# First stage of a SiLU MLP forward and backward: how the first 512 rows of x reach their transposed tile, and which queue loads the first slices of w1

## The chip, the cores and the metric

One NeuronCore of a Trainium2 chip runs the kernel. TensorE (PE) multiplies 128x128 weight tiles with up to 512 moving columns into PSUM; VectorE (DVE), ScalarE (ACT) and GpSimd (POOL) work beside it; SyncE (SP) does no arithmetic here and issues DMAs. A DMA can be issued from SP's queue or from ScalarE's. The metric is the device time of one execution in microseconds (us), the median of several runs, lower being better. Times inside the kernel are counted from the start of the profiled span.

## What is computed

x is 2048 x 640 (S x D), w1 is 640 x 1536 (D x F), w2 is 1536 x 640, all bf16. The reference is the forward pass and its gradients by x, w1 and w2 for a given grad_out:

```python
h = x @ w1
a = silu(h)
out = a @ w2
# and, from grad_out:
ga  = grad_out @ w2.T
gh  = ga * silu'(h)
gx  = gh @ w1.T
gw1 = x.T @ gh
gw2 = a.T @ grad_out
```

## The kernel before, in words

The rows are worked in NCH = 4 chunks of SC = 512. For a chunk the kernel needs x transposed (`xT`, 128 partitions x 5 blocks of D x 512 rows) and grad_out transposed (`goT`). With 128 of the 1536 columns of F as one group, `h_group` (L226) forms h with five matmuls (one for each block `dt_` of D, L206), takes silu (`silu_a`, L215, ScalarE), and prepares the derivative (`silu_grad`: tanh on ScalarE, L219, then two VectorE instructions, L221 and L222). `g_group` (L250) does the same for grad_out with w2 transposed. `sd_phase` (L264) multiplies back to D: w2 with a for `out`, w1 transposed with gh for `gx`. Intermediate results go to DRAM and come back transposed by DMA (`store_rows`, `load_a_blk`), and after the chunks the weight gradients gw2 (L357) and gw1 (L406) are accumulated over all rows. All of that is as it was.

What matters here is the first stage, chunk 0. Its order is this:

- **Warm-up.** `warm` is filled by VectorE (L141) and NWARM = 22 matmuls of 128 columns run on it (L145), before any data has come.
- **Loads on SP's queue, in this order.** Two loads of 256 rows of x each, whole rows, into `x_two` (`load_x_half`, L173, 320 KB each); w1's first 512 columns (the first of three slices of F) in three pieces, rows 0 to 127, rows 128 to 255 and the other three blocks (`load_w1_rows`, L178: 128, 128 and 384 KB); the second and third slice of w1 (`load_w1`, L169, 640 KB each); all of w2 (L186, 1920 KB); then DMA transposes of grad_out (L162), w2 (L189) and w1 (L190).
- **`start_before_entry_wait` (L16).** The instructions named in `early` (the warm-up, the two loads of x and the first two of w1), with all that stands ahead of them on their engine, are moved in front of the wait with which each engine enters the program proper. Each engine signals its arrival before them, so another engine does not wait for them.
- **ScalarE's table load.** A first activation of one column (L185) makes ScalarE load its function table.
- **Transposes on TensorE.** `pe_x_half` (L192) turns each half of the 512 rows: for each of the five blocks of D two transposes (L197) into one PSUM tile, then one copy to `xT` (L199), on VectorE for even `dt_` and on ScalarE for odd ones. Rows were loaded two to a partition, so the copy spreads them with a stride. In all 20 transposes and 10 copies.
- **`h_first` (L232).** For the first four groups (FB = 4, the first slice of w1) the first KM = 2 blocks of D are multiplied ahead, block by block over the four groups; then each of these groups is completed with the remaining blocks, and the other eight groups follow, five matmuls each. The fifth group is the first to need the second slice of w1. Each group's silu follows it, its tanh LAG_G = 4 groups later in the text.
- **Then** `sd_phase` with w2 and `aT`, the twelve `g_group`s of chunk 0 and `sd_phase` with w1T.

PSUM has eight buffers under one tag (`hp`), taken in turn by the warm-up tile, the transposed pieces and the groups. [...] The tanh result has three buffers (`tpool`), each freed by the VectorE instruction that reads it (L221).

The program's order on an engine can differ from the text, since a scheduler places instructions.

Of the kernel before, what the change touches and what calls it, by code (L numbers as in the profile page):

```python
# [9 lines left out]
ACT = mybir.ActivationFunctionType  # L10
# [5 lines left out]
def start_before_entry_wait(nc, names):  # L16

    def move(nc):
        blocks = nc.m.functions[0].blocks
        entry, home = blocks[0].instructions, blocks[1].instructions
        for engine in {i.engine for i in home if i.name in names}:
            mine = [i for i in home if i.engine == engine]
            last = max(k for k, i in enumerate(mine) if i.name in names)
            moved = mine[: last + 1]
            gate = next(
                k
                for k, i in enumerate(entry)  # L30
                if i.engine == engine and isinstance(i, mybir.InstEventSemaphore)
            )
            taken = {i.name for i in moved}
            for k in reversed(range(len(home))):
                if home[k].name in taken:
                    del home[k]
            for i in reversed(moved):
                entry.insert(gate, i)

    nc.at_finalize(move)  # L40
# [22 lines left out]
def kernel(  # L63
# [11 lines left out]
    nc = tc.nc  # L75
    P = 128
    x2 = x.flatten_outer_dims()
# [5 lines left out]
    S, D = x2.shape  # L83
    F = w1.shape[1]
    ST, DT, FT = S // P, D // P, F // P
    SC = 512
    NCH = S // SC
    STC = SC // P
    FC = 512
# [1 line left out]
    FB = FC // P  # L91
    LAG = 2
    LAG_G = 4
    KM = 2
    NWARM = 22
    dt_in = x.dtype

    dram = ctx.enter_context(tc.tile_pool(name="dram", bufs=1, space=bass.MemoryType.DRAM))
# [13 lines left out]
    w1_v = w1.rearrange("(dt p) f -> p dt f", p=P)  # L112
    w2_v = w2.rearrange("(ft p) d -> p ft d", p=P)
    x_v = x2.rearrange("(st p) d -> p st d", p=P)
# [17 lines left out]
    with ExitStack() as mctx:  # L132
        cpool = mctx.enter_context(tc.tile_pool(name="cpool", bufs=1))
# [6 lines left out]
        warm = cpool.tile([P, P], dt_in, name="warm")  # L140
        early = [nc.vector.memset(warm[:], 1.0)]  # L141
        warm_a = cpool.tile([P, 1], FP32, name="warm_a")
        wp = ps_h.tile([P, SC], FP32, name="wp", tag="hp")
        for i in range(NWARM):
            early.append(nc.tensor.matmul(wp[:, 0:P], lhsT=warm[:], rhs=warm[:], start=True, stop=True))  # L145

        ident = cpool.tile([P, P], dt_in, name="ident")
        make_identity(nc, ident[:])

        w1_nat = w1pool.tile([P, DT, F], dt_in, name="w1_nat", tag="w1a")  # L150
# [4 lines left out]
        def load_xT(c):  # L155
            xT = xpool.tile([P, DT, SC], dt_in, name="xT")
            nc.sync.dma_start_transpose(out=xT[:], in_=x2[c * SC:(c + 1) * SC, :])
            return xT
# [4 lines left out]
            return goT  # L163

        xT_next = xpool.tile([P, DT, SC], dt_in, name="xT")
        x_two = cpool.tile([P, 2, 2, D], dt_in, name="x_two")

        def load_w1(lo, hi):
            nc.sync.dma_start(out=w1_nat[:, :, lo:hi], in_=w1_v[:, :, lo:hi])  # L169

        def load_x_half(half):
            lo = half * 2 * P
            return nc.sync.dma_start(  # L173
                out=x_two[:, half, :, :], in_=x2[lo:lo + 2 * P, :].rearrange("(p q) d -> p q d", q=2)
            )

        def load_w1_rows(lo, hi):
            return nc.sync.dma_start(out=w1_nat[:, lo:hi, 0:FC], in_=w1_v[:, lo:hi, 0:FC])  # L178

        early += [load_x_half(0), load_x_half(1), load_w1_rows(0, 1), load_w1_rows(1, KM)]  # L180
        load_w1_rows(KM, DT)
        start_before_entry_wait(nc, {i.ins.name for i in early})
        for fc in range(1, NFC):
            load_w1(fc * FC, (fc + 1) * FC)
        nc.scalar.activation(warm_a[:], warm[:, 0:1], ACT.Silu)  # L185
        nc.sync.dma_start(out=w2_nat[:], in_=w2_v[:])  # L186
        goT_next = load_goT(0)
        for fc in range(NFC):
# [1 line left out]
        nc.sync.dma_start_transpose(out=w1T[:], in_=w1[:, :])  # L190

        def pe_x_half(xT, half):  # L192
            lo = half * 2 * P
            for dt_ in range(DT):
                tp = ps_h.tile([P, 2, P], dt_in, name="tp", tag="hp")
                for q in range(2):
                    nc.tensor.transpose(tp[:, q, :], x_two[:, half, q, dt_ * P:(dt_ + 1) * P], ident[:])  # L197
                copy = nc.scalar.copy if dt_ % 2 else nc.vector.tensor_copy
                copy(out=xT[:, dt_, lo:lo + 2 * P].rearrange("p (s q) -> p q s", q=2), in_=tp[:])  # L199

        pe_x_half(xT_next, 0)
        pe_x_half(xT_next, 1)

        def h_mm(hp, ft, xT, lo, hi):
            for dt_ in range(lo, hi):
                nc.tensor.matmul(  # L206
                    hp[:],
                    lhsT=w1_nat[:, dt_, ft * P:(ft + 1) * P],
                    rhs=xT[:, dt_, :],
                    start=(dt_ == 0),  # L210
                    stop=(dt_ == DT - 1),
                )
# [19 lines left out]
        def h_first(xT, aT, ghT):  # L232
            hps = []
            for ft in range(FB):
                hps.append(ps_h.tile([P, SC], FP32, name="hp"))
            for dt_ in range(KM):
                for ft in range(FB):
                    h_mm(hps[ft], ft, xT, dt_, dt_ + 1)
            for i in range(FT + LAG_G):
                if i < FT:  # L240
                    if i < FB:
                        h_mm(hps[i], i, xT, KM, DT)
                    else:
# [40 lines left out]
        for c in range(NCH):  # L284
            xT, goT = xT_next, goT_next
# [3 lines left out]
            if c + 1 < NCH:  # L289
                xT_next = load_xT(c + 1)  # L290
# [8 lines left out]
            if c == 0:  # L299
                h_first(xT, aT, ghT)  # L300
                nc.sync.dma_start(
                    out=aT_scr[:, c * SC:(c + 1) * SC].rearrange("(ft p) s -> p ft s", p=P), in_=aT[:]
                )
                sd_phase(c, w2_nat, aT, oT_scr)
                for ft in range(FT):
                    g_group(ft, goT, ghT)
                nc.sync.dma_start(
                    out=ghT_scr[:, c * SC:(c + 1) * SC].rearrange("(ft p) s -> p ft s", p=P), in_=ghT[:]
# [4 lines left out]
            for i in range(FT + LAG):  # L313
# [7 lines left out]
                out=aT_scr[:, c * SC:(c + 1) * SC].rearrange("(ft p) s -> p ft s", p=P), in_=aT[:]  # L321
            )
            nc.sync.dma_start(
                out=ghT_scr[:, c * SC:(c + 1) * SC].rearrange("(ft p) s -> p ft s", p=P), in_=ghT[:]
# [7 lines left out]
    with ExitStack() as fctx:  # L332
# [45 lines left out]
        for fc in range(NFC):  # L378
            gh_blk = gh_blks[fc]
            for dt_ in range(DT):  # L380
                if dt_ == DT // 2:
                    store_gw2(fc)
                if fc == NFC - 1 and dt_ == DT - 1:
                    for k, (lo, hi) in enumerate(((0, FC - P), (FC - P, FC))):
# [12 lines left out]
                        else:  # L397
                            nc.vector.tensor_copy(out=g1[:, lo:hi], in_=gp[:, lo:hi])  # L398
                        last_store = nc.sync.dma_start(
                            out=gw1_v[:, dt_, fc * FC + lo:fc * FC + hi], in_=g1[:, lo:hi]  # L400
# [49 lines left out]
```

## Time and profile before

| what | value |
|---|---|
| median of 5 runs | 320.91 us (320.52 to 321.57) |
| the profiled execution, its own time | 320.68 us |
| its span in the profile | 318.9 us |
| outside the span | 1.8 us |
| PE busy | 315.4 us, 1498 matmuls and as many weight loads |
| VectorE, ScalarE, GpSimd busy | 102.5, 77.8, 0.7 us |
| moved by DMA | 67.33 MB, mean 211 GB/s |
| TensorE clock granted | 0.999 of full speed |

The profile page gives busy times by engine, the span in 40 slices, the chain of work that ended last (followed back from the last instruction to what released each step), groups of instructions by line, and DMA issues with the time from issue to landing. The trace behind it can be asked for stretches: a timeline of merged instructions, the chain within a window, engine use within windows, and the DMAs issued within a window. An SPq row is SyncE's queue: its duration is how long SP took to issue, not to move. The time to landing counts from the start of the issue. A row "L206 PE MATMUL hp<-xT,w_nat" is the matmul of line 206 that reads `xT` and `w1_nat` and writes a PSUM tile; names are shown without digits, so `w_nat` stands for w1 and for w2. Matmuls overlap, so that the duration of one (379 ns) is longer than the distance to the next.

### The profile page before, as it was taken

What the parts mean: (1) busy time and instruction counts of PE and PEld (TensorE: products, weight loads), DVE (VectorE), ACT (ScalarE), POOL (GpSimd) and SP (SyncE); (2) the same over time, 40 slices, a digit from 0 to 9 for tenths busy, and PEclk for the clock granted to TensorE, in tenths of its full rate; (3) what the DMA queues carried; (4) which work ended last, traced back from release to release, by engine and by line L of the source; (5) the groups of instructions that cost most, each with busy time, mean ns of one, the idle gap of its engine ahead of it and who ended that gap; (6) DMA issues with size and microseconds to landing.
All of it is one profiled execution on the core that took longest, in us unless ns stands there. A gap on an engine that the chain in (4) does not pass through costs nothing.

```text
span 318.9 us, 3570 instructions
## 1 busy us (share of the span) xinstructions
PE 315.4 (99%) x1498; PEld 145.8 (46%) x1498; DVE 102.5 (32%) x182; ACT 77.8 (24%) x142; POOL 0.7 (0%) x6
## 2 busy tenths in 40 slices
PE   8999999999999999999999999999999999999996
PEld 6444444444444444444444444444444444444443
DVE  3871641477410187710147741000000100001001
ACT  4951000644201354311064420111100001001100
POOL 0000000000000000000000000000000000000000
PEclk9999999999999999999999999999999999999999
DMA  8999999999999855282644089819999998995111
GB/s 272 328 177 232 240 305 254 342 245 288 276 290 288 220 183 151 99 296 82 167 123 123 2 268 265 210 32 292 264 204 275 258 254 295 248 294 184 38 38 44
DMA packets 147311, 67.33 MB, mean 211 GB/s; under 512 B 112608, under 2 KB 147040, under 8 KB 147296
## 3 DMA queue, kind: packets, MB, share of 16 engines
q1 hardware_dynamic: 147296, 67.12, 80.7%
q8 instruction: 11, 0.18, 0.2%
q14 instruction: 4, 0.03, 0.0%
HBM read 9.83 MB, written 28.97 MB: 122 GB/s over the span
## 4 chain that ended last, share of the span: by engine, by line
PE 98%; DMA 1%; DVE 1%; issue 0%; DVEq 0%; SPq 0%
PE hp L269 32%; PE hp L206 16%; PE hp L253 16%; PE hp L357 16%; PE hp L406 15%; PE hp L387 1%; DMA x_two<-in_x_dram 1%; DVE xT L199 1%; PE tp L197 0%; DVE g L398 0%; DVEq L398 0%; SPq L434 0%
## 5 line engine op out<-in xcount | busy, mean ns | idle before, releaser
L206 PE MATMUL hp<-xT,w_nat 128*128 128x512 bf16 x240 | 56.9, 379 | 0.2 <-DVE xT L199 0.2
L253 PE MATMUL hp<-goT,w2T 128*128 128x512 bf16 x240 | 56.9, 379 | 0.0
L269 PE MATMUL hp<-aT,w_nat 128*128 128x512 bf16 x240 | 52.5, 379 | 0.0
L269 PE MATMUL hp<-ghT,w1T 128*128 128x512 bf16 x240 | 52.5, 379 | 0.0
L357 PE MATMUL hp<-a_blk,go_nat 128*128 128x512 bf16 x240 | 52.0, 379 | 0.0
L406 PE MATMUL hp<-gh_blk,x_nat 128*128 128x512 bf16 x224 | 48.5, 379 | 0.0
L277 ACT ACTIVATE oT<-hp 128x512 bf16<-128x512 f32 x24 | 14.3, 597 | 109.8 <-PE hp L269 109.8
L215 ACT ACTIVATE aT<-hp 128x512 bf16<-128x512 f32 x48 | 30.0, 627 | 32.8 <-PE hp L206 32.8
L206 PEld LDWEIGHTS <-w_nat 128*128 128x128 bf16 x240 | 23.5, 98 | 28.4 <-issue 0.3
L269 PEld LDWEIGHTS <-w_nat 128*128 128x128 bf16 x240 | 23.5, 98 | 28.3
L253 PEld LDWEIGHTS <-w2T 128*128 128x128 bf16 x240 | 23.5, 98 | 28.3
L357 PEld LDWEIGHTS <-go_nat 128*128 128x128 bf16 x240 | 23.5, 98 | 28.3
L269 PEld LDWEIGHTS <-w1T 128*128 128x128 bf16 x240 | 23.4, 98 | 28.4
L279 DVE CAST oT<-hp 128x512 bf16<-128x512 f32 x16 | 11.1, 692 | 77.0 <-PE hp L269 77.0
L260 DVE SCALAR_TENSOR_TENSOR ghT<-ghT,hp 128x512 bf16<-128x512 bf16 x48 | 32.5, 681 | 7.3 <-PE hp L253 7.3
L406 PEld LDWEIGHTS <-x_nat 128*128 128x128 bf16 x224 | 21.9, 98 | 26.4
L222 DVE SCALAR_TENSOR_TENSOR ghT<-aT,v 128x512 bf16<-128x512 bf16 x48 | 32.8, 686 | 0.5
L221 DVE TENSOR_SCALAR v<-t 128x512 bf16<-128x512 f32 x48 | 20.3, 426 | 30.1 <-ACT t L219 30.1
L219 ACT ACTIVATE t<-hp 128x512 f32<-128x512 f32 x48 | 29.9, 628 | 0.0
L417 DVE CAST g<-hp 128x512 bf16<-128x512 f32 x7 | 4.8, 692 | 47.1 <-PE hp L406 27.7
L367 DVE CAST g2T<-hp 128x512 bf16<-128x512 f32 x7 | 4.8, 691 | 46.1 <-PE hp L357 46.1
L365 ACT ACTIVATE g2T<-hp 128x512 bf16<-128x512 f32 x8 | 4.8, 597 | 47.0 <-PE hp L357 47.0
(20 smaller groups left out, 26.0 us busy)
## 6 DMA issues: line engine op xcount, KB each, us to landing
aT_scr<-aT SPq DMA_DIRECT2D x4, 1536.0 KB, 6.2
ghT_scr<-ghT SPq DMA_DIRECT2D x4, 1536.0 KB, 8.2
out_dram<-o_sb SPq DMA_DIRECT2D x8, 640.0 KB, 3.6
oT_scr<-oT SPq DMA_DIRECT2D x4, 640.0 KB, 3.6
go_nat<-in_grad_out_dram SPq DMA_DIRECT2D x4, 640.0 KB, 6.5
x_nat<-in_x_dram SPq DMA_DIRECT2D x4, 640.0 KB, 5.4
gxT_scr<-oT SPq DMA_DIRECT2D x4, 640.0 KB, 4.7
w_nat<-in_w_dram SPq DMA_DIRECT2D x1, 1920.0 KB, 12.3
```

Of the source, the lines that this page charges most:

```text
L206: nc.tensor.matmul(hp[:], lhsT=w1_nat[:, dt_, ft * P:(ft + 1) * P], rhs=xT[:, dt_, :], start=(dt_ == 0), stop=(dt_ == DT - 1),)
L215: nc.scalar.activation(aT[:, ft, :], hp[:], ACT.Silu)
L219: nc.scalar.activation(t[:], hp[:], ACT.Tanh, scale=0.5)
L221: nc.vector.tensor_scalar(out=v[:], in0=t[:], scalar1=-0.5, scalar2=0.5, op0=ALU.mult, op1=ALU.add)
L222: nc.vector.scalar_tensor_tensor(out=ghT[:, ft, :], in0=aT[:, ft, :], scalar=1.0, in1=v[:], op0=ALU.subtract, op1=ALU.mult)
L253: nc.tensor.matmul(gp[:], lhsT=w2T[:, dt_, ft * P:(ft + 1) * P], rhs=goT[:, dt_, :], start=(dt_ == 0), stop=(dt_ == DT - 1),)
L260: nc.vector.scalar_tensor_tensor(out=ghT[:, ft, :], in0=ghT[:, ft, :], scalar=1.0, in1=gp[:], op0=ALU.add, op1=ALU.mult)
L269: nc.tensor.matmul(op_[:], lhsT=w_all[:, ft, dt_ * P:(dt_ + 1) * P], rhs=rhs_all[:, ft, :], start=(ft == 0), stop=(ft == FT - 1),)
L277: nc.scalar.activation(oT[:, dt_, :], op_[:], ACT.Copy)
L279: nc.vector.tensor_copy(out=oT[:, dt_, :], in_=op_[:])
L357: nc.tensor.matmul(gp[:], lhsT=go_nat[:, st, dt_ * P:(dt_ + 1) * P], rhs=a_blk[:, st, :], start=(st == 0), stop=(st == ST - 1),)
L406: nc.tensor.matmul(gp[:], lhsT=x_nat[:, st, dt_ * P:(dt_ + 1) * P], rhs=gh_blk[:, st, :], start=(st == 0), stop=(st == ST - 1),)
```

## The change

The first 512 rows of x no longer come whole. Columns 0 to 255 (two blocks of D, KT = 2) are loaded in two halves of 256 rows, now with row p of a block on partition p, and are transposed on TensorE as before, by 8 transposes and 4 copies. Columns 256 to 639 (three blocks) are brought by one DMA transpose straight into `xT`, issued on SP's queue behind the two loads. The three pieces of w1's first slice go to ScalarE's queue, rows 0 to 127, rows 128 to 255 and the other three blocks as before; the activation that loads the table stands ahead of them in the text. In the built program ScalarE's order is: first piece, table load, activation, second piece, third piece, all in front of the entry wait. KM becomes 3 and NWARM 20.

```diff
-    KM = 2
-    NWARM = 22
+    KM = 3
+    NWARM = 20
+    KT = 2
...
-        x_two = cpool.tile([P, 2, 2, D], dt_in, name="x_two")
+        x_first = cpool.tile([P, STC, KT * P], dt_in, name="x_first")
...
         def load_x_half(half):
-            lo = half * 2 * P
-            return nc.sync.dma_start(
-                out=x_two[:, half, :, :], in_=x2[lo:lo + 2 * P, :].rearrange("(p q) d -> p q d", q=2)
-            )
+            rows = slice(2 * half, 2 * half + 2)
+            return nc.sync.dma_start(out=x_first[:, rows, :], in_=x_v[:, rows, 0:KT * P])
 
         def load_w1_rows(lo, hi):
-            return nc.sync.dma_start(out=w1_nat[:, lo:hi, 0:FC], in_=w1_v[:, lo:hi, 0:FC])
-
-        early += [load_x_half(0), load_x_half(1), load_w1_rows(0, 1), load_w1_rows(1, KM)]
-        load_w1_rows(KM, DT)
+            return nc.scalar.dma_start(out=w1_nat[:, lo:hi, 0:FC], in_=w1_v[:, lo:hi, 0:FC])
+
+        early += [load_x_half(0), load_x_half(1)]
+        early.append(nc.sync.dma_start_transpose(out=xT_next[:, KT:DT, :], in_=x2[0:SC, KT * P:D]))
+        nc.scalar.activation(warm_a[:], warm[:, 0:1], ACT.Silu)
+        early += [load_w1_rows(0, 1), load_w1_rows(1, 2), load_w1_rows(2, DT)]
         start_before_entry_wait(nc, {i.ins.name for i in early})
         for fc in range(1, NFC):
             load_w1(fc * FC, (fc + 1) * FC)
-        nc.scalar.activation(warm_a[:], warm[:, 0:1], ACT.Silu)
...
         def pe_x_half(xT, half):
-            lo = half * 2 * P
-            for dt_ in range(DT):
+            for dt_ in range(KT):
                 tp = ps_h.tile([P, 2, P], dt_in, name="tp", tag="hp")
                 for q in range(2):
-                    nc.tensor.transpose(tp[:, q, :], x_two[:, half, q, dt_ * P:(dt_ + 1) * P], ident[:])
+                    nc.tensor.transpose(tp[:, q, :], x_first[:, 2 * half + q, dt_ * P:(dt_ + 1) * P], ident[:])
                 copy = nc.scalar.copy if dt_ % 2 else nc.vector.tensor_copy
-                copy(out=xT[:, dt_, lo:lo + 2 * P].rearrange("p (s q) -> p q s", q=2), in_=tp[:])
+                copy(out=xT[:, dt_, half * 2 * P:(half + 1) * 2 * P], in_=tp[:])
```

## The prediction

> **What bounds the kernel now.** I read the page first: is there any engine but TensorE that could set the end?
>
> ```profile
> span 318.9 us, 3570 instructions
> PE 315.4 (99%) x1498; PEld 145.8 (46%) x1498; DVE 102.5 (32%) x182; ACT 77.8 (24%) x142; POOL 0.7 (0%) x6
> PE 98%; DMA 1%; DVE 1%; issue 0%; DVEq 0%; SPq 0%
> ```
>
> TensorE is busy 315.4 of 318.9 us, and the chain that ended last is 98% TensorE. What is not TensorE lies at the start, so I asked for the chain of waits within the first 30 us:
>
> ```profile
> 0.08 3.00 DMA x_two<-in_x_dram
> 3.08 0.05 issue
> 3.13 0.41 PE tp L197 x2
> 3.56 1.64 DVE xT L199 x4
> 5.20 0.04 issue
> 5.25 13.11 PE hp L206 x60
> 18.36 11.65 PE hp L269 x54
> ```
>
> The first real matmul starts at 5.25 us: the first half of x lands at 3.08, two transposes, four VectorE copies. The 60 matmuls of h then run without a gap: the next stage starts at 18.19, so (18.19 - 5.25)/60 = 0.2157 us a matmul. After 5.25 TensorE never stops (every stage in its timeline begins where the one before ends), so whatever moves the end of the h stage moves the end of the kernel.
>
> The second question is what else is late in the first 10 us. The timeline of SP's queue, then the DMAs issued from 2.3 to 2.7 us (the last column of these is us to landing):
>
> ```profile
> 0.08 0.87 SPq L173 DMA_DIRECT2D x_two<-in_x_dram  x2
> 0.99 1.44 SPq L178 DMA_DIRECT2D w_nat<-in_w_dram  x3
> 2.48 1.06 SPq L169 DMA_DIRECT2D w_nat<-in_w_dram  x2
> 3.58 0.60 SPq L186 DMA_DIRECT2D w_nat<-in_w_dram  x1
> 4.22 13.09 SPq L162 DMA_TRANSPOSE goT<-in_grad_out_dram  x1
> ```
>
> ```profile
> w_nat<-in_w_dram SPq DMA_DIRECT2D x1, 640.0 KB, 6.3
> w_nat<-in_w_dram SPq DMA_DIRECT2D x1, 384.0 KB, 4.1
> ```
>
> The second slice of w1 (640 KB) lands at 2.48 + 6.3 = 8.78 us. The fifth group needs it, after 20 matmuls: 5.25 + 20 x 0.2157 = 9.57. So it has only 0.8 us to spare: a start earlier by more than that meets this load. The same view gives 3.9 for the second half of x, 4.3 and 4.9 for the first pieces of w1, and about 6.1 for the third.
>
> The third question is whether the DMA engines have room. Engine use in windows (last columns: clock, DMA share, GB/s):
>
> ```profile
> 2.00:3.00 1.00, 1.00 (x10) 0.77 (x8) 0.00 (x0) 0.22 (x2) 0.00 (x0) 1.00 0.98 340
> 4.00:5.00 1.00, 1.00 (x14) 0.91 (x13) 1.00 (x4) 0.93 (x3) 0.00 (x0) 1.00 0.86 292
> 5.00:6.00 1.00, 0.78 (x5) 0.38 (x4) 0.86 (x3) 0.48 (x2) 0.00 (x0) 1.00 0.93 268
> 7.00:8.00 1.00, 1.00 (x6) 0.46 (x5) 0.00 (x0) 0.18 (x1) 0.00 (x0) 1.00 1.08 367
> ```
>
> They move nothing before about 1 us and are nearly full after that. The bytes that must come ahead of the fifth group are the same in both kernels: 640 + 640 + 640 KB before; 256 + 384 (transposed) + 640 + 640 KB after.
>
> **The change, step by step.** *Warm-up.* 22 matmuls last 2.53 us, some 0.107 apart; two fewer end at about 2.83 instead of 3.04. Nothing waits for them but the transposes, which can start near 2.65.
>
> *Halves of x.* 128 KB instead of 320. The first load's 3.00 us to landing held about 1 us of start, 0.9 of moving 320 KB at 340 GB/s and the rest at its end. 128 KB take 0.4, or 0.8 where w1's first piece shares the engines: landing at 2.4 to 2.75, I take 2.7. The second half, issued 0.4 later, lands near 3.1.
>
> *Transposes and copies.* Before, four VectorE copies at 0.44 stood in a row ahead of the first matmul. After, block 0 has two, one to a half; block 1 goes by ScalarE beside them. From 2.75: two transposes 0.41, copy to 3.62; the second half's block was transposed in between, its copy ends at 4.1. First matmul **4.15** (4.0 to 4.5), 1.1 us earlier. The stride that the copies lose I cost at nothing; a VectorE copy of half the columns took 0.29 (L398), which bounds the gain at some 0.15 each.
>
> *w1 on ScalarE's queue.* Piece one leaves at about 0.1 us and lands by 2.7 to 3.4, ahead of 4.15. Pieces two and three stand behind the table load (1.28 us) and the activation (0.20). If issuing waits for these, they leave at about 2.05 and 2.45; if not, at 0.95 and 1.35. No row shows a DMA issued by ScalarE; from SP such a load took 3.3 to 3.5 (128 KB) and 4.1 (384 KB) with 640 to 900 KB ahead of it. Now less is ahead: piece two by 4.5 to 5.5 against a need at 4.15 + 4 x 0.2157 = 5.0; piece three between 5.4 and 6.55, I take 6.2, nearest to the 4.1 row. ScalarE's copies of block 1 are queued behind these issues, ready at 3.4 while the issues end by 2.9: covered by 0.5 us.
>
> *The DMA transpose.* 384 KB, three fifths of a 640 KB one. Of those, the w2T ones took 3.18 us to issue and 5.9 to land, the o_sb ones (also a column slice) 2.55 and 4.7, the fastest xT 3.07 and 6.1. Scaling the issue and keeping the tail (2.2 to 3.0): 3.7 to 4.9 after an issue at 0.95, so 4.65 to 5.8 when undisturbed; I take 5.6. The disturbed ends of the trace are far off (below).
>
> *KM = 3.* Eight matmuls (blocks 0 and 1 of four groups) need neither the DMA transpose nor piece three: cover until 4.15 + 1.73 = 5.88. Then 12 matmuls of the first slice. Block 2 starts at the latest of 5.88, 5.6 and 6.2: **6.2**, a wait of 0.3.
>
> *Second slice of w1.* SP reaches it after the transpose's issue of 1.5 to 1.9 us, at 2.5 to 2.9: 0 to 0.4 later than 2.48. Same bytes ahead: 8.8 to 9.2. Two queues may fill what is unused from 4 to 6.5 (share 0.86 to 0.94, 0.25 us): 8.5. A transpose that holds back others by its slower rate (384 KB at 640 KB per 3.18 us against 340 GB/s) costs 0.7: up to 9.6. I take 8.85.
>
> *Sum.* The fifth group can start at max(6.2 + 12 x 0.2157, 8.85) = max(8.79, 8.85), say 8.87, against 9.57: **0.7 us earlier**, where the start had promised 1.1.
>
> *Behind it.* With KM = 3 ScalarE gets its first group after 14 matmuls, not 11: 6.2 + 5 x 0.2157 + 0.38 = 7.66, near 7.82 of before. In the changed order four silus run before the first tanh, at 0.49 each, so VectorE's L221/L222 pairs (0.43 + 0.69 = 1.11) start at about 10.2, not 8.93. Tanh number n waits for pair n - 3: the last silu, behind tanh 10 and so behind pair 7 (10.2 + 7 x 1.11 + 0.43), ends near 19.6. It is needed by the twelfth matmul of the next stage, 8.87 + 8.63 + 2.37 = 19.87. Covered by 0.3 us; if not, the excess is lost. w2 (landed at 15.9) is needed at 17.5. grad_out's transpose (20.2 against 31.1) and all later loads have spare microseconds. The end of the program is the same.
>
> So the profiled 320.68 becomes 319.98 (span 318.2), and the median, 0.23 above that execution, **320.2**.
>
> **Rules weighed.** The row: the DMA engines' share is 0.98 at 2 to 3 us. [...]
>
> The row: the transposes last 314 ns until about 4.2 us and 219 from 4.4, though the granted clock stands at 1.00 throughout. [...]
>
> **Rivals.** *The start pays in full*: piece three and the second slice land by 5.9 and 8.5. Gain 1.1: 319.8. For it: two queues; against it: full engines.
>
> *Given back*: the second slice lands at 9.2 to 10, or block 2 waits to 7 (7 + 2.59 is 9.57, the break-even): 320.6 to 321.3. For it: the slack of only 0.8 us, the slower transpose.
>
> *Slower: the DMA transpose is late because copies share its engines.* Disturbed transposes of the trace land after 10.3 (an xT) or 11.4 (median goT); three fifths of it from 0.95 is 7.1 to 7.8. Decides from 6.98 on; at 7.8 the fifth group starts at 10.4: +0.8, 321.7. Against it: little is ahead of it here, while goT's 16.0 stood behind 1920 KB.
>
> *The half-speed stretch lasts longer.* TensorE idles from 3.7 to 4.15; if the 3.8 us (0.51 to 4.3) began anew, 8.8 matmuls would take the time of 17.6: fifth group at 10.37, also 321.7.
>
> **How the numbers follow.** Forecast (gain 0.4 to 0.95) 0.47; in full 0.13; given back 0.20; late transpose 0.15; half speed 0.05. Some 0.2% (0.64 us) is about what a measurement can tell. Faster by more: 0.13 + 0.38 of the forecast = 0.51; within: 0.09 + 0.18 + 0.02 = 0.29; slower: 0.20. Range 319.6 to 321.6: from the full gain to near the late transpose.
>
> **What would show it.** First matmul near 4.15; a wait of L205 for the DMA transpose or for w1 at block 2, 0 to 0.7 us; the fifth group at 8.5 to 9.2; then no gap. Wrong if TensorE waits more than 1.1 us in all after its first matmul, if the early matmuls stand 0.43 apart, or if the sixty end later than 18.19.

## The result

The changed kernel is slower: 321.91 us median of 30 runs (321.21 to 322.62) against 320.97 of 53 runs of the kernel before, a ratio of 1.0028 (95% interval 1.0022 to 1.0033). The forecast was 320.2. The profiled executions are 321.97 and 320.68 us, 1.3 apart, as are their spans.

The page of the changed kernel: span, TensorE, and the chain that ended last.

```profile
span 320.2 us, 3540 instructions
PE 316.4 (99%) x1484; PEld 145.0 (45%) x1484; DVE 100.3 (31%) x178; ACT 76.9 (24%) x140; POOL 0.7 (0%) x6
PE 97%; DMA 2%; SPq 0%; DVE 0%; issue 0%; DVEq 0%
```

TensorE is "busy" 1.0 us longer with 14 matmuls fewer, and DMA has 2% of the chain instead of 1%. The chain within the first 35 us (start, length, what) says which DMA:

```profile
1.09 7.15 DMA xT<-in_x_dram
8.24 0.04 issue
8.29 11.38 PE hp L205 x52
19.67 12.95 PE hp L268 x60
```

The path no longer runs over the halves of x, but over the DMA transpose, which lands at 8.24 us, 7.15 after its issue began. Only the 52 matmuls from block 2 on stand behind it; the eight before it are not on the chain at all. By the distance of 0.2157 us, the fifth group starts at 8.29 + 12 x 0.2157 = 10.88 instead of 9.57: 1.31 late, which is the 1.3 us of the span. The next stage starts at 19.51 instead of 18.19, and behind it nothing else is lost.

Three rows of the timeline show what the chain leaves out.

```profile
0.63 1.28 ACT L181 ACT_TABLE_LOAD   x1 [0.63 <-POOLq L433]
0.69 0.89 ACTq L177 DMA_DIRECT2D w_nat<-in_w_dram  x2
4.49 3.57 PE L205 MATMUL hp<-xT,w_nat 128*128 128x512 bf16 x8 [0.17 <-DVE xT L198]
```

ScalarE issues its second and third piece of w1 (the ACTq row) while its table is still loading: they leave at 0.7 and 1.1 us and share the DMA engines with x: from 1 to 2 us ScalarE's queue has 13.5% of the engines' time and SyncE's 44.4%. And the first eight matmuls, from 4.49 on, stand 0.427 us apart, half the usual rate: 8 x 0.427 ends them at 7.9, so that only 0.2 us of the wait for the DMA transpose shows as idle. The "busy" time hides it.

Last, the DMAs issued from 1.0 to 1.4 us (KB, us to landing), and engine use from 1 to 6 us, first of this kernel, then of the kernel before (the last columns are clock, DMA share, GB/s).

```profile
w_nat<-in_w_dram ACTq DMA_DIRECT2D x1, 384.0 KB, 5.9
xT<-in_x_dram SPq DMA_TRANSPOSE x1, 7.2
```

```profile
1.00:6.00 5.00, 4.54 (x30) 2.89 (x28) 0.58 (x2) 1.86 (x4) 0.29 (x1) 1.00 1.00 183
```

```profile
1.00:6.00 5.00, 4.68 (x44) 3.93 (x42) 2.29 (x6) 2.85 (x6) 0.29 (x1) 1.00 0.92 300
```

By their share the DMA engines are as busy as before, yet they move 183 GB/s instead of 300. The second queue is not the whole of that: the run spq below, with one queue, moves 201. From 5 to 6 us this kernel moves only 80 GB/s; why stays open.

The time of the DMA engines can be split by queue. From 3.6 to 4.2 us (packets, MB, and the time that the packets took as a share of the 16 engines, which can add up to over 100%; q10 is ScalarE's queue, q1 SyncE's):

```profile
q10 hardware_dynamic: 114, 0.12, 91.2%
q1 hardware_dynamic: 66, 0.02, 12.4%
```

All 66 packets of SyncE's queue are under 512 bytes, so they are the transpose's, whose issue had ended at 3.4. It moves 0.02 MB while w1's pieces, on the other queue, move 0.12. From 6 to 8 us it is the other way round: 0.06 MB on ScalarE's queue, 0.48 on SyncE's, most of its packets of that small size (1352 of the 1559 packets of both queues).

### The profile page after: what moved, and what is told of

Its sections match the earlier page's. It is cut to its first block, busy times and chain, and to the rows that moved or that the text cites. A ratio compares the mean times of both kernels' runs of the same rounds, so it can differ in the third digit from the quotient of the medians.

```text
span 320.2 us, 3540 instructions
## 1 busy us (share of the span) xinstructions
PE 316.4 (99%) x1484; PEld 145.0 (45%) x1484; DVE 100.3 (31%) x178; ACT 76.9 (24%) x140; POOL 0.7 (0%) x6
## 4 chain that ended last, share of the span: by engine, by line
PE 97%; DMA 2%; SPq 0%; DVE 0%; issue 0%; DVEq 0%
PE hp L268 32%; PE hp L252 16%; PE hp L356 16%; PE hp L205 16%; PE hp L405 15%; DMA xT<-in_x_dram 2%; PE hp L386 1%; SPq L174 0%; DVE g L397 0%; DVEq L397 0%; SPq L433 0%
## 5 line engine op out<-in xcount | busy, mean ns | idle before, releaser
L205 PE MATMUL hp<-xT,w_nat 128*128 128x512 bf16 x240 | 58.7, 387 | 0.4 <-DMA xT<-in_x_dram 0.2
```

The lines of the kernel that those rows point to most:

```text
L205: nc.tensor.matmul(hp[:], lhsT=w1_nat[:, dt_, ft * P:(ft + 1) * P], rhs=xT[:, dt_, :], start=(dt_ == 0), stop=(dt_ == DT - 1),)
```

## The experiments

The theories: **A**, the late DMA transpose sets the time, with A1 (the pieces of w1 on the other queue hold it up), A2 (a slice of 384 columns is slow by itself), A3 (the loads queued behind it slow it); **B**, the half-rate stretch sets the time. Where a time is given with a ratio, it is against the kernel before on the same chip; the ratio is worked out over all runs and can differ a little from that of the two medians. Landings are those of one profiled execution of each run, and loads that are issued alike do not land alike in every execution: the second slice of w1 lands at 8.8 us in the kernel before and at 10.2 in cold.

### What holds the DMA transpose up

**The pieces of w1 behind it on SyncE's queue (spq).** This run also splits a later, undisturbed DMA transpose, far off the path.

```diff
-            return nc.scalar.dma_start(out=w1_nat[:, lo:hi, 0:FC], in_=w1_v[:, lo:hi, 0:FC])
+            return nc.sync.dma_start(out=w1_nat[:, lo:hi, 0:FC], in_=w1_v[:, lo:hi, 0:FC])
```

> The changed kernel with the three pieces of w1 on SyncE's queue, behind the DMA transpose; nothing runs on ScalarE's queue. Far off the path, the second chunk's DMA transpose of x is split into 256 and 384 columns, which times such a slice by itself. Theory A1 (copies of the other queue share the DMA engines and hold the transpose up): it lands 3.7 to 4.9 us after its issue, near 5 to 6, while the pieces of w1 land later than 6. Theory A2 (a slice of 384 columns is slow by itself): it still takes 7 us to landing, and so does the slice of the second chunk. If it takes 7 here and 4 to 5 in the second chunk, neither holds.

The DMAs issued near 1.1 us, and SyncE's queue near 37 us:

```profile
xT<-in_x_dram SPq DMA_TRANSPOSE x1, 3.9
```

```profile
37.03 1.58 SPq L160 DMA_TRANSPOSE xT<-in_x_dram  x1
```

It lands 3.9 us after its issue, near 5.0: A1. The later slice takes 1.58 us to issue, the early one 1.66 here, but 2.34 in the changed kernel: the slice as such is as fast as forecast (3.9 us to landing against 3.7 to 4.9), and A2 falls. The single execution took 321.59 us, since w1's first piece now lands only at 5.8, its third at 7.8 and the second slice at 10.5: TensorE waits for these instead.

**All later loads of SyncE's queue held until it has landed (hold).** GpSimd copies one element of its result into each later target, which the loads then overwrite.

```diff
+        landed = xT_next[:, DT - 1, SC - 1:SC]
+        for h in held:
+            nc.gpsimd.tensor_copy(out=h, in_=landed)
```

> The changed kernel with all later loads of SyncE's queue (slices 2 and 3 of w1, w2, and what follows) held until the DMA transpose has landed, by GpSimd copies of one element from its result into their targets, which the loads then overwrite. The time will be worse, since those loads come late; the landing of the transpose is what counts. Theory A3 (the loads queued behind it slow it): 3.7 to 4.9 us to landing. Theories A1 and A2: 7 us as in the changed kernel.

```profile
xT<-in_x_dram SPq DMA_TRANSPOSE x1, 6.8
```

With nothing queued behind it the transpose still takes 6.8 us: A3 accounts for at most 0.4. (The single execution took 325.83 us, because the second slice of w1 comes late, as intended.)

**Only the third piece of w1 behind it on SyncE's queue (third_sp).**

```diff
+            queue = nc.sync if lo == 2 else nc.scalar
+            return queue.dma_start(out=w1_nat[:, lo:hi, 0:FC], in_=w1_v[:, lo:hi, 0:FC])
```

> The changed kernel with only the third piece of w1 (384 KB) moved to SyncE's queue behind the DMA transpose; 256 KB stay on ScalarE's queue instead of 640. Theory A1: the transpose lands between the 3.9 us after issue of the run without a second queue and 7.2, near 5 (so at 6 us), and block 2 then starts when the third piece lands, 7 to 7.5: the time 320.9 to 321.4. If the two small pieces hold the transpose as much as all three did, it lands at 8.2 and the time stays at 321.9.

```profile
xT<-in_x_dram SPq DMA_TRANSPOSE x1, 4.6
```

With 0, 256 and 640 KB on the other queue the DMA transpose lands 3.9, 4.6 and 7.2 us after its issue (4.7 and 7.2 again in the two runs with fillers below). That follows A1. The time does not: 323.01 us, ratio 1.0064 (1.0051 to 1.0076), slower than the changed kernel although the transpose is 2.5 us earlier. The chain of this run:

```profile
5.04 7.30 PE hp L206 x21
12.35 0.05 issue
12.40 8.37 PE hp L206 x38
```

21 matmuls take 7.3 us: until 10.3 they stand 0.427 apart. Block 2 could have started when the third piece landed, at 7.7 to 8.0, so that at the full rate the fifth group would have started at 10.4; it did at 12.0. That points to theory B, and the next two runs price it.

### What the half rate costs

**The same with TensorE kept busy (third_fill).** Filler matmuls read the half that has just landed and write the warm-up tile; their result is not used.

```diff
-    NWARM = 20
+    NWARM = 24
...
+        def fill(half, n):
+            for _ in range(n):
+                nc.tensor.matmul(wp[:, 0:P], lhsT=ident[:], rhs=x_first[:, 2 * half, 0:P], start=True, stop=True)
         pe_x_half(xT_next, 0)
+        fill(0, 6)
         pe_x_half(xT_next, 1)
+        fill(1, 5)
```

> The run with only the third piece of w1 on SyncE's queue (323.01 us, slower than the changed kernel although its DMA transpose landed at 5.7 instead of 8.2), with 24 warm-up matmuls and filler matmuls after the transposes of each half, so that TensorE idles less ahead of its first real matmul. There the matmuls stood 0.427 us apart from 5.0 to about 10.3 us. If the half-rate stretch is what it lost: the rate doubles by 4.5 to 7 us, block 2 starts when the third piece has landed, near 7.8, the fifth group near 10.4 instead of 12.1, and the time is 321.2 to 321.6. If something else held it: no change, 323.0.

```profile
7.95 10.53 PE hp L212 x48
```

The rate doubles near 6 us, block 2 waits for its load until 7.95, and the next stage starts at 19.18 instead of 20.60. The time falls from 323.01 to 321.71 us (ratio to before 1.0022, 1.0009 to 1.0035). With less idling ahead of the first real matmul that kernel is 1.3 us faster.

**The changed kernel with TensorE kept busy (fill).** The same with 22 warm-up and 3 and 3 filler matmuls.

> The changed kernel with 22 warm-up matmuls and three filler matmuls after the transposes of each half, so that TensorE has no idle stretch before its first real matmul. In the changed kernel the first eight matmuls stand 0.427 us apart, not 0.216, and the DMA transpose lands at 8.24 us. Theory A (the late DMA transpose sets the time): the eight matmuls stand 0.216 apart, end near 6.3, TensorE then waits some 1.9 us, the other 52 start at 8.3 as before, and the time stays at 321.9. Theory B (the half-rate stretch sets it): 0.9 us less, 321.0. If the spacing stays 0.427, an idle stretch is not what keeps the rate low.

```profile
5.28 2.46 PE L211 MATMUL hp<-xT,w_nat 128*128 128x512 bf16 x8
8.30 4.91 PE L211 MATMUL hp<-xT,w_nat 128*128 128x512 bf16 x21 [0.56 <-DMA xT<-in_x_dram]
```

The second half of x landed at 4.5 in this execution, so that TensorE still idled 0.6 us, and the rate doubled only near 6.5; but the eight matmuls end half a microsecond ahead of the transpose, and the 52 start at 8.30 against 8.29. The time is 321.94 us, ratio 1.0024 (1.0013 to 1.0035), as for the changed kernel. In the changed kernel theory A sets the time, and B's price is hidden under the same wait.

**The kernel before with 6 warm-up matmuls (cold).**

```diff
-    NWARM = 22
+    NWARM = 6
```

> The kernel before with 6 warm-up matmuls instead of 22, so that TensorE idles from about 1.2 to 3.1 us; nothing else. It prices the half-rate stretch by itself, with loads as before. If an idle stretch puts off the full rate: the transposes stay at 0.107 apart, the first matmul starts near 5.4, matmuls stand 0.427 apart until some point between 5.3 and 8.5 us, and the time is 0.3 to 1.7 us worse. If the full rate comes at 4.3 us whatever TensorE did before: no difference.

```profile
5.52 6.66 PE hp L206 x23
```

The matmuls stand 0.427 apart from 5.3 to about 8.7 us; the next stage starts at 20.00 instead of 18.19 in the profiled execution (322.49 us). The loads are issued as before, but the second slice landed at 10.2 here: at the full rate the fifth group would have waited until then instead of starting at 9.57, and it started at 11.4. So the half rate takes 1.2 of the 1.8 us. The median is 321.63, ratio 1.0027 (1.0014 to 1.0039), and the runs lie in two groups, 321.1 to 321.6 and 322.1 to 322.5; that the point of doubling differs between them is likely, but only one execution has a trace.

The gaps alone do not fix that point. The run plain, below, has the changed kernel's program up to its first matmuls; TensorE idles 0.27 and 0.18 us ahead of its two groups of transposes (0.21 us ahead of the transposes in the changed kernel), and yet its rate doubles at 3.9 us. In x3, with a gap of 0.36 us, it doubles at 4.7; in third_fill, where TensorE has no gap from 0.50 to 7.4 us, only near 6. So an idle stretch of this size is neither enough for a late doubling nor needed for one; what decides in a single execution is not shown.

### What the second queue and the shorter rows do to plain loads

**The kernel before with w1's pieces on ScalarE's queue, nothing else (actq).**

```diff
-            return nc.sync.dma_start(out=w1_nat[:, lo:hi, 0:FC], in_=w1_v[:, lo:hi, 0:FC])
+            return nc.scalar.dma_start(out=w1_nat[:, lo:hi, 0:FC], in_=w1_v[:, lo:hi, 0:FC])
```

> The kernel before with one part of the change alone: the three pieces of w1 on ScalarE's queue, around its table load; x comes in whole rows as before and all five blocks are transposed on TensorE. Theory A1 in its wide form (two queues at once move less than one, whatever they carry): the second half of x lands at 4.5 or later, not 3.9, the second slice of w1 after 9.6, not 8.78, and the time is 0.3 to 1.5 us worse than before, 321.3 to 322.5. Narrow form (only a DMA transpose, or rows of 512 to 768 bytes, suffer from the other queue): landings within 0.3 us of before, time within 0.5 us of 321.0.

The chain, the second slice of w1 in the DMAs issued near 1.1 us, and engine use:

```profile
0.54 5.38 DMA x_two<-in_x_dram
```

```profile
w_nat<-in_w_dram SPq DMA_DIRECT2D x1, 640.0 KB, 7.8
```

```profile
1.00:6.00 5.00, 3.19 (x31) 2.75 (x29) 1.20 (x3) 1.96 (x4) 0.29 (x1) 1.00 0.95 304
```

The second half of x lands 5.4 us after its issue, at 5.92 instead of 3.9, and the first matmul starts at 6.79. Yet the engines move 304 GB/s, as before (300), and the second slice lands at 1.08 + 7.8 = 8.9, as before (8.78). So the wide form of A1 was wrong in its reason: here a second queue does not make them move less, it takes the order away. From 2.3 to 2.6 us, with x still under way, ScalarE's queue has more of the engines than SyncE's:

```profile
q10 hardware_dynamic: 72, 0.06, 63.2%
q1 hardware_dynamic: 19, 0.03, 46.2%
```

x does not wait for all of the other queue: the second half of x lands at 5.9 us, w1's second piece at 6.1, its third only at 8.4. Of x's 256 packets of 2560 bytes 9 moved from 4 to 5 us and 2 from 5 to 6; why these came so late stays open. Both queues move packets in the same stretch, with 63.2% and 46.2% of the engines' time here and 91.2% and 12.4% in the changed kernel from 3.6 to 4.2 us; what divides the engines between the queues is not shown. This part of the change alone costs more than the whole change: 322.24 us, ratio 1.0046 (1.0033 to 1.0059).

**Columns 256 to 639 by a plain load in the transpose's place, twelve more transposes on TensorE (plain), and the same on one queue (col_sp).**

```diff
-        early.append(nc.sync.dma_start_transpose(out=xT_next[:, KT:DT, :], in_=x2[0:SC, KT * P:D]))
+        early.append(nc.sync.dma_start(out=x_rest[:], in_=x_v[:, 0:STC, KT * P:D]))
```

> The changed kernel without the DMA transpose: columns 256 to 639 come by one plain load in its place, and TensorE transposes them (12 more transposes) between the matmuls of block 0 and those of block 1. Theory A: the load lands by 4.5 to 5.5, no wait of more than 0.3 us is left, and the fifth group starts near 4.5 + 20 x 0.216 + 0.66 + 0.3 = 9.8, so 321.2. Theory B: matmuls and transposes up to about 7.7 us go at half rate and lose 1.6 us, so 322.8, slower than the changed kernel.

> No DMA transpose and no DMA on ScalarE's queue: on SyncE's queue the two halves of 256 columns, two pieces of w1, columns 256 to 639 by a plain load, the third piece, then as before. TensorE transposes the last three blocks between the matmuls of block 0 and block 1. It has the rows of 512 and 768 bytes that the run with the plain load on two queues had, but one queue. Theory A1 (two queues): the 384 KB land 3.5 to 4.5 us after their issue, near 5.5 to 6, not 7.1 after it, the second slice near 8.8, and the time is 320.5 to 321.3. Rival (short rows are slow): the 384 KB still take 6 to 7 us, and the time is over 322.5.

The load of 384 KB, first on two queues, then on one:

```profile
x_rest<-in_x_dram SPq DMA_DIRECT2D x1, 384.0 KB, 7.1
```

```profile
x_rest<-in_x_dram SPq DMA_DIRECT2D x1, 384.0 KB, 3.8
```

A plain load lands as late beside the other queue as the transpose did, 7.1 against 3.8 us, so the delay is not peculiar to transposing. The course is another, though: from 3.5 to 4 us SyncE's queue here has 59% of the engines and ScalarE's 18%, so it is not shown that one and the same thing holds both up. On two queues TensorE then idled 2.7 us and fell back to half rate, which here the granted clock shows too (its column is the third from the end):

```profile
7.00:8.00 1.00, 0.00 (x0) 0.00 (x0) 0.00 (x0) 0.00 (x0) 0.00 (x0) 0.62 1.06 354
8.00:9.00 1.00, 0.72 (x8) 0.72 (x8) 0.08 (x1) 0.00 (x0) 0.00 (x0) 0.50 1.08 379
```

It stays at 0.50 up to 14 us, and the time is 326.26 us, ratio 1.0163 (1.0147 to 1.018): my expectation of theory B, 322.8, was far too small, since it had no wait in it. On one queue it is 321.75 us, ratio 1.0037 (1.002 to 1.0055), also worse than expected. The 384 KB land near 5.9, as said, but twelve transposes and 16 matmuls come behind them (5.92 + 0.69 + 16 x 0.2157 = 10.06 for the fifth group), which my expected time did not add up; and the second slice of w1 lands only at 3.20 + 7.0 = 10.2, not 8.8. From 1 to 6 us this kernel moves about 245 GB/s against 300, on one queue and without a DMA transpose; what differs from the kernel before is one more load and rows of 512 and 768 bytes instead of 2560. Which of the two it is was not separated; rows as short as that are not needed for it, since x3, below, with one more load and rows of 1280 bytes, moves 246.

### Attempts at a faster version

**x's rows one to a partition, copies without a stride (rows); x's first half in two loads (x3); the kernel before with three fillers ahead of its first matmul (before_fill).** The load of rows; the copies' order is changed to match, and the edits of the other two are as the expectations say:

```diff
-                out=x_two[:, half, :, :], in_=x2[lo:lo + 2 * P, :].rearrange("(p q) d -> p q d", q=2)
+                out=x_two[:, half, :, :], in_=x_v[:, 2 * half:2 * half + 2, :]
```

> The kernel before with x's halves loaded with row p of a block on partition p (1280 contiguous bytes, not 2560), so that the copies write without a stride; nothing else. In the changed kernel such a copy took 0.29 us on VectorE instead of 0.44. Expected of it: the four copies take 1.2 instead of 1.64 us, the first matmul waits for the end of the 20 transposes, near 5.0 instead of 5.25, and the time is 0.2 us better, 320.6, unless the shorter rows make the halves land later by as much.

> The kernel before with x's first 256 rows in two loads of 128 rows (whole rows of 1280 bytes), the copies without a stride, the first 256 rows copied five blocks at once (one copy on VectorE, one on ScalarE), and 20 warm-up matmuls; all on SyncE's queue. It starts the transposes earlier without a second queue, a DMA transpose or short rows. Expected: the first 128 rows land near 2.4 us, transposes from 2.7, first matmul at 4.7 to 4.9; the second slice of w1 lands near 9.2, the fifth group starts at 9.1 to 9.3 instead of 9.57: 320.5 to 320.8. If the earlier pieces cost SyncE's queue more than that, the second slice lands after 9.6 and the time is over 321.0.

> The kernel before with 23 warm-up matmuls and three filler matmuls between its last transpose and its first real matmul, where TensorE idles 0.2 us; loads as before. The runs so far show that an idle stretch ahead of the first matmul can put off the doubling of TensorE's rate, and that the kernel before has runs near 320.7 and others near 321.3. If those of the second kind are runs in which the rate doubled late because of its short gaps, most runs now fall near 320.7 and the median is 0.2 us better than before; if the gaps do not matter, no difference.

None beats the kernel before. rows: 321.41 us, ratio 1.0006 (0.9992 to 1.0019). Its copies are shorter (three in 1.15 us), but the second half landed at 4.6 instead of 3.9 in the profiled execution, and the rate doubled only near 6.9. x3: 321.49 us, ratio 1.0023 (1.0006 to 1.004), though its profiled execution, 320.70 us, is level with before: the first 128 rows land at 2.4 as expected, the second half at 4.2. before_fill: 320.89 us, ratio 1.0011 (0.9998 to 1.0024). What makes the runs of the kernel before fall near 320.7 or near 321.3 stays open.

## Why the prediction was wrong

**The step that failed is the landing of the DMA transpose**: 5.6 us forecast, 8.24 measured, so that block 2 started at 8.29 instead of 6.2. Its undisturbed price was right (3.7 to 4.9 us from issue to landing forecast, 3.9 measured in spq). Wrong was to take the undisturbed price, while three pieces of w1 with 640 KB ran beside it on the other queue. I had the rival with that mechanism, at 0.15, for a landing of 7.1 to 7.8; it was priced at +0.8 and came to +1.3 (profiled executions), because the landing was later still. What I held against it, that little is queued ahead of it, does not count: what runs beside it decides (0, 256 and 640 KB: 3.9, 4.6 and 7.2 us). That the other queue holds the transpose up is shown; why SyncE's queue gets so little of the engines is not.

**The other queue's bytes.** I wrote that the same bytes stand ahead of the fifth group, and priced the second slice by their total. In actq that total does land at the same time (8.9 us); but the order was what the kernel before lived on. There x (3.1 and 3.9 us), then w1's pieces (4.3, 4.9 and 6.1), then its slices (8.8 and 10.6) landed one after another, the first of these slices 0.8 us ahead of its need. With two queues the second half of x landed together with w1's second piece (5.9 and 6.1 us in actq).

**When the pieces leave.** Of the two cases, behind the table load (2.05 and 2.45 us) or not waiting for it (0.95 and 1.35), the second held, and earlier yet: 0.7 and 1.1. I took the early issue for a gain of the third piece; it also put w1's pieces beside x and the DMA transpose almost from the start (no run holds them back to 2.05). The third piece landed at 1.1 + 5.9 = 7.0 instead of 6.2 all the same, and by my own sum that alone puts the fifth group at 7.0 + 2.59 = 9.6, level with before.

**First matmul.** 4.49 against 4.15: the first half of x took 2.9 us to landing instead of 2.6, and the second landed at 3.7 instead of 3.1; in spq, with nothing on the other queue, the first took 2.2 us and the second landed at 3.4. The copies were cheaper than I took them, 0.29 instead of 0.44 us, at the bound that I had named.

**Half rate.** The rival at 0.05 did occur (0.427 us from 4.49 to 7.9), and would have cost about what it was priced at (4.49 + 8 x 0.427 + 12 x 0.2157 = 10.5 for the fifth group); here it cost nothing, since the DMA transpose came later still. The rate doubled at 3.9 us in plain, 4.3 in the kernel before, near 6 and 6.5 in the runs with fillers, 8.7 in cold and 10.3 in third_sp. That idling makes the 3.8 us (0.51 to 4.3) begin anew, on which the rival rested, was my estimate, and no run shows it: plain, with gaps of 0.27 and 0.18 us, doubles earlier than third_fill without.

**Second slice of w1.** 10.1 us (3.58 + 6.5) against 8.85: SyncE came to it 0.7 us later than the latest I had allowed, as the disturbed transpose took 2.34 us to issue. It too would have undone the gain (9.57 was the need before) and is hidden under the transpose. So by these sums the late transpose, the half rate, the second slice and the third piece would each have sufficed to take the forecast gain away; only the first shows in the time.

**What was right.** The early stage alone decides and everything after 19.5 us follows; the silu and VectorE work behind KM = 3 stayed covered (the last silu starts at 20.28 us, needed at 19.51 + 2.37 = 21.88).

## What to carry to other kernels

Ask of a load that is moved to a second queue not when it is issued, but which loads it will now run beside: in these runs loads on one queue landed in the order of issue (in the kernel before from 3.1 us, x, to 15.9, w2), while beside a second queue an urgent load landed up to 3.3 us later (7.2 against 3.9 us after its issue). When a wait is removed at the start of a kernel, list everything that was just in time behind it; here the third piece, the second slice and the DMA transpose all came in between 7.0 and 10.1 us. And look at the distance between matmul starts, not only at busy time: a stretch at half rate counts as busy and can hide a wait (here TensorE was busy for 316.4 us with 1484 matmuls, against 315.4 with 1498).

## What the runs showed that was not expected

- ScalarE's sequencer issues DMAs during its own table load: the load runs from 0.63 to 1.91 us, the two issues from 0.69 to 1.6.
- The doubling of TensorE's rate came at 3.9 to 4.7 us in some runs (plain, actq, before, x3) and at 6 to 10.3 us in others (6.5 in fill, 10.3 in third_sp), with idle gaps of 0.1 to 0.4 us ahead of that point in the one kind and of none (third_fill) to 1.9 us (cold) in the other. At the start the granted clock in the profile stands at 1.00 while the rate is half (matmuls 0.427 us apart, not 0.2157, from 4.49 to 7.9 in the changed kernel); after 2.7 us of idling (plain) it does show 0.50.
- A load's landing moves with its neighbours by more than a factor of 1.8: 384 KB took 3.8 or 7.1 us plain, 3.9 or 7.2 transposed.
